# Attention with chunk selection and a gated MLP block: weight loads tied to pairs 2 and 3, six weight and four activation transposes moved from DMA to TensorE, evacuations on either engine, a new order table

## The chip, the cores and the metric

One NeuronCore of a Trainium2 chip runs the whole program. The metric is device time in microseconds (us) from the first to the last instruction and what the launch adds. The kernel before took 241.61 us as the median of 3 runs (240.44 to 242.94).

## The reference

```python
# attention: B=4, H=8, S=768, D=64, chunk=32 (24 chunks), top_k=6
k_min, k_max = per-chunk minimum and maximum of k over its 32 rows
ub = np.sum(np.maximum(q * k_min, q * k_max), axis=-1)          # a bound for each query and chunk
ub = np.where(causal, ub, -1e9)
top_chunks = np.argsort(ub, axis=-1)[..., -top_k:]
scores = np.where(sel & causal_by_position, (q @ k.T) / sqrt(D), -1e9)
attn_out = softmax(scores) @ v
# gated MLP on x = attn_out as (B, S, 512)
h = gelu_tanh(x @ w_in)                                        # w_in 512 x 1024
u, v = h[..., :512], h[..., 512:]
v_n = (v - mean) / sqrt(var + 1e-6) * g_ln                     # over the 512 features
v_s = einsum('ts,bsd->btd', w_sg, v_n) + b_sg[None, :, None]   # w_sg 768 x 768, over positions
out = x + (u * v_s) @ w_out                                    # w_out 512 x 512
```

Inputs and output are float32; the kernel multiplies in bf16 behind the selection.

## The kernel before, in words

**Units of work.** The 32 heads (4 batches of 8) go in 16 pairs, p0 to p15; four pairs are a batch, and each batch ends in the MLP. A function makes named operations, and each is a few instructions on one engine. For a pair: `lk`, `lq`, `lv` load k, q, v of one head each by DMA from SyncE (192 KB, in pieces of 256 bytes, at most four of them in flight). `kt` and `qt` are TensorE transposes into PSUM. `kn` and `kx` (VectorE) take the chunk minima and maxima, `ke`, `ka`, `kb` and `qe` (ScalarE) copy the transposed k and q out of PSUM, `qr` is the positive part of q, and `qa`, `qb`, `qc` (GpSimd) are bf16 casts of q. `ub` multiplies for the bounds of one selection group: pair 0, pair 1, then pairs two at a time. `ut`, `uc`, `um`, `ud`, `uq` (all VectorE) transpose, cut off what is not causal, find the sixth largest, compare, and transpose back: they make the mask. `s` multiplies scores into one of two PSUM tiles PSC, `e` (ScalarE) takes the exponential out of it, `af` (GpSimd) cuts the diagonal, `pv` and `pd` multiply by v, and `xr`, `xs` (VectorE) normalise into XS. Pairs 0 to 3 (batch 0) use tiles of both heads (`s0.3`, `e0.3`); later heads have three tiles each (`s8h.0`). There the mask rows reach QA and QB by small DMAs `d`.

**The MLP of a batch.** `xt` makes x^T of 128 features from XS: a DMA transpose on SyncE (line 824), except for the last of batch 3, which TensorE makes (line 833). Then come `hv` and `gv` (v half and gelu), `bs`, `ba`, `re`, `rp`, `vh` (the norm), `hu` and `gu` (u half and gelu), `pt` (the product with w_sg), `vs`, `gm` (scaling and gating; `gm` on GpSimd or VectorE), `ou`, `oa`, `os` (out product, residual, store).

**Weights.** `win` (w_in, 4 DMAs, line 489), `wsg` (w_sg, 6, line 493) and `wo` (w_out, 4, line 500) are loads with a cast that GpSimd issues. `wsgT` (line 496) are six DMA transposes on SyncE that make w_sg^T. The w_sg staging tile lies in the buffer that the first gelu writes.

**Order.** `ORDER` is a table written out by hand: one list of all operations, from which each engine takes its own in turn. `kt0.0:0` names a PSUM buffer, `qr0@act` an engine other than the default. An engine runs its list strictly in order, and waits on semaphores for what an operation reads, for the users of the PSUM buffer that it takes over, and for tiles to come free. The instructions that follow in its list wait with it, on SyncE's and GpSimd's DMA queues too. Operations that share a PSUM tile run in the order in which the program made them. `FILL` puts a number of multiplications of a zero tile `warm` (line 984) before a TensorE operation that waits; they need only the PSUM buffer, and keep TensorE at work.

The plan has one stretch that repeats: attention for the next pairs runs between the products of the MLP of the batch before. Batch 0 has no such partner: until the first `hv0`, TensorE has only batch 0's attention and the first operations of pairs 4 to 8.

## Time and profile before

| | |
|---|---|
| runs, median (lowest to highest) | 241.61 us (240.44 to 242.94) |
| the profiled execution, its own time | 239.15 us |
| its span, first to last instruction | 237.4 us |
| busy: TensorE, VectorE, ScalarE, GpSimd | 211.3, 175.1, 167.3, 107.1 us |
| granted TensorE clock, mean | 0.995 |

Busy time is the time in which at least one instruction of the engine ran; matmuls are pipelined, so TensorE's includes their tails, and it includes the `warm` multiplications. PEld is TensorE's weight load. In the views, a line number is that of the printed kernel; tiles are named by the program, and as `KP` lies in the buffer of `uT`, and the w_sg staging in that of `vgb`, their rows carry those names.

### The profile page before, as it was taken

The numbers are of one execution on the slowest core, as the hardware profiler recorded it, in microseconds if no ns is written. First come the engines' busy times: TensorE is split into PE (matmuls) and PEld (weight loads), VectorE is DVE, ScalarE is ACT, GpSimd is POOL, SyncE is SP. The second block draws the span as 40 slices with busy tenths as digits, with TensorE's granted clock in tenths as the row PEclk, the third lists the DMA queues.
The fourth block names the chain that finished last, engine by engine and source line by source line (L and its number), as shares of the span: only waits on it lengthen the run. The fifth ranks groups of instructions, "written<-read, shape, count | busy, mean of one in ns | idle before, by whom it ended". The sixth has DMA issues, their size and how long they took to land.

```text
span 237.4 us, 6067 instructions
## 1 busy us (share of the span) xinstructions
PE 211.3 (89%) x2329; PEld 133.2 (56%) x2351; DVE 175.1 (74%) x543; ACT 167.3 (70%) x264; POOL 107.1 (45%) x147
## 2 busy tenths in 40 slices
...
GB/s 160 207 219 192 204 207 209 200 195 171 123 209 177 182 199 147 81 95 216 195 227 177 186 26 82 134 166 69 4 94 30 92 123 79 196 140 0 0 90 176
DMA packets 100541, 33.72 MB, mean 142 GB/s; under 512 B 93985, under 2 KB 96801, under 8 KB 100513
## 3 DMA queue, kind: packets, MB, share of 16 engines
...
q8 instruction: 18, 0.29, 0.5%
...
## 4 chain that ended last, share of the span: by engine, by line
PE 65%; DVE 14%; ACT 12%; DMA 4%; issue 2%; POOL 0%; POOLq 0%; SPq 0%; DVEq 0%; ACTq 0%
PE PSG L909 11%; PE PSC L775 9%; PE PSG L889 9%; PE PSG L854 8%; PE PSG L932 5%; PE PSG L796 5%; DVE W L535 4%; PE PSG L528 3%; ACT E L745 3%; PE PSG L623 3%; PE PSG L984 3%; PE PSG L561 3%; ACT E L779 2%; DMA xT<-XS 2%; ACT qT L567 2%
## 5 line engine op out<-in xcount | busy, mean ns | idle before, releaser
L779 ACT ACTIVATE E<-PSC 128x1024 bf16<-128x1024 f32 (+1 forms) x72 | 62.8, 916 | 11.3 <-PE PSC L775 10.9
L681 POOL TENSOR_SCALAR_AFFINE_SELECT E<-E 128x768 bf16<-128x768 bf16 (+3 forms) x40 | 29.3, 745 | 27.1 <-ACT E L779 19.3
L535 DVE TENSOR_REDUCE W<-PSG 128x12 f32<-128x384 f32 x64 | 34.4, 547 | 9.2 <-PE PSG L528 8.6
L909 PE MATMUL PSG<-wsgT,vhat 128*128 128x384 bf16 x192 | 35.2, 326 | 1.5 <-DVE XS L815 1.4
L745 ACT ACTIVATE E<-PSC 128x1024 bf16<-128x1024 f32 (+3 forms) x26 | 21.7, 858 | 7.5 <-PE PSC L735 7.2
L916 DVE SCALAR_TENSOR_TENSOR vsT<-PSG,glnT,bsgbc 128x384 f32<-128x384 f32 x32 | 18.9, 604 | 9.1 <-PE PSG L909 7.4
L909 PEld LDWEIGHTS PSG<-wsgT,vhat 128*128 128x128 bf16 x192 | 17.9, 98 | 12.7 <-DVE XS L815 1.6
L586 POOL CAST vx<-vn 128x768 bf16<-128x768 f32 x16 | 13.4, 843 | 22.2 <-DMA vn<-in_v_dram 21.9
L854 PE MATMUL PSG<-winb,xT 128*128 128x512 bf16 x93 | 21.9, 379 | 1.4 <-ACT qT L567 0.9
L922 POOL TENSOR_TENSOR uT<-vsT,uT 128x384 bf16<-128x384 f32 x17 | 16.0, 947 | 14.9 <-DVE vsT L916 14.8
L889 PE MATMUL PSG<-xT,winb 128*128 128x384 bf16 x128 | 22.3, 326 | 0.4 <-DMA xT<-XS 0.3
L932 PE MATMUL PSG<-woutb,uT 128*128 128x512 bf16 x86 | 21.7, 379 | 0.9 <-POOL uT L922 0.3
L874 POOL TENSOR_TENSOR rstd<-rstd,neghalf 128x3 f32<-128x3 f32 x8 | 7.6, 948 | 32.9 <-DVE rstd L870 32.9
L796 PE MATMUL PSG<-vx,E 128*128 128x65 bf16 x480 | 19.7, 194 | 1.5 <-DVE osb L939 1.4
L567 ACT ACTIVATE qT<-PSG 128x384 f32<-128x384 f32 x32 | 15.3, 496 | 8.2 <-PE PSG L561 7.8
L775 PE MATMUL PSC<-QA,KA 96*128 96x128 bf16 (+2 forms) x168 | 19.3, 246 | 1.7 <-ACT qT L567 0.9
L939 DVE TENSOR_TENSOR osb<-PSG,XS 128x512 f32<-128x512 f32 x24 | 16.2, 686 | 5.7 <-DMA out_dram<-osb 4.4
L796 PEld LDWEIGHTS PSG<-vx,E 128*128 128x128 bf16 x480 | 17.7, 98 | 4.0 <-DVE osb L939 1.8
L813 DVE RECIPROCAL rden<-PSG 128x6 f32<-128x6 f32 x32 | 6.0, 189 | 18.3 <-PE PSG L804 18.2
L775 PE MATMUL PSC<-QB,KB 128*128 128x128 bf16 (+2 forms) x168 | 19.3, 246 | 0.1
L864 DVE BATCH_NORM_STATS2 stats<-vgb 128x6 f32<-128x512 f32 x24 | 15.9, 682 | 4.0 <-ACT vgb L859 3.9
L984 PE MATMUL PSG<-warm 128*128 128x512 bf16 x45 | 14.0, 430 | 5.3 <-ACT qT L567 1.6
...
## 6 DMA issues: line engine op xcount, KB each, us to landing
...
```

The lines of the kernel that those rows point to most:

```text
L535: P.op(f"k{'nx'[m]}{p}.{hf}", "dve", lambda d, t=t, m=m, op=op, hf=hf: d.tensor_reduce(W[w][:, m, 12 * hf:12 * hf + 12], t.ap()[:, 0:TG].r ...
L567: P.op(f"qe{p}.{hf}", "act", lambda e, t=t, cs=cs: e.activation(qT[w][:, cs], t.ap()[:, 0:TG], ACTF.Copy), writes=[("qT", w, hf)], ps=[t], ...
L681: P.op(f"af{h}.{r}", "pool", lambda g, ev=ev, cnt=cnt: g.affine_select(ev, ev, pattern=[[0, cnt], [1, 128]], compare_op=ALU.is_ge, fill=0. ...
L745: P.op(f"e{p}.{c}", "act", lambda e, t=t, o0=o0, nn=nn: e.activation(E[:, slot:slot + 2, o0:o0 + nn], t.ap().rearrange("p (i x) -> p i x", ...
L775: r = e.matmul(t.ap()[:, o:o + n], kt_[rows, 128 * kb:128 * kb + 128], qt_[rows, q0:q0 + n], start=True, stop=True, skip_group_check=True)
L779: P.op(f"e{h}h.{c}", "act", lambda e, t=t, c0=c0, c1=c1: e.activation(E[:, es, c0:c1], t.ap()[:, 0:c1 - c0], ACTF.Exp, scale=SCALE), write ...
L796: r = e.matmul(t.ap()[:, 65 * qb:65 * qb + 65], E[:, es, a:a + 128], vx[w][:, kb, i, :], start=first, stop=False, skip_group_check=True)
L854: r = e.matmul(t.ap()[:, 0:F], xT[s][:, dk, 128 * qt:128 * qt + 128], winb[:, dk, F:DFF], start=(dk == 0), stop=(dk == NDK - 1))
L889: r = e.matmul(t.ap()[:, 0:TG], winb[:, dk, 128 * fb:128 * fb + 128], xT[s][:, dk, TG * tg:TG * tg + TG], start=(dk == 0), stop=(dk == NDK ...
L909: r = e.matmul(t.ap()[:, 0:TG], vhat[s][:, sb, 128 * fb:128 * fb + 128], wsgT[:, sb, TG * tg:TG * tg + TG], start=(sb == 0), stop=(sb == N ...
L932: r = e.matmul(t.ap()[:, 0:DM], gT[s][:, fb, 128 * qt:128 * qt + 128], woutb[:, fb, :], start=(fb == 0), stop=(fb == NF - 1))
L984: return e.matmul(o.ps[0].ap()[:, 0:512], warm[:, 0:128], warm[:], start=True, stop=True, skip_group_check=True)
```

## The change

What it does:

- **Weight loads.** `win`, `wsg`, `wo`, `bsg`, `gln` are now made after pair 3's operations and each waits for one: `win0` and `win1` for `qc2`, `win2` and `win3` for `qc3`, `wsg0` to `wsg5` for the exponentials `e2.0` to `e2.5`, `wo`, `bsg`, `gln` for those of pair 3.
- **w_sg^T by TensorE.** Each of six staged blocks of w_sg goes through six transposes into a PSUM tile (`wt`), and a VectorE copy of 128x768 bf16 (`we`). The six DMA transposes on SyncE are gone. The staging lies in `vhat[1]` and `xT[1]`, buffers of batch 1.
- **x^T of batch 0 by TensorE.** `XPE` now lists the four `xt0`, so four more DMA transposes are gone. The copy out of PSUM is one operation of 768 columns (`xe`), on VectorE or ScalarE, where batch 3's last had been one of 384 on each.
- **Evacuations.** `ke`, `ka`, `kb`, `qe`, `xe` may run on either engine. In the new table 15 of them that ScalarE had run stand on VectorE (`ka6.1`, `kb5.1` and `ka6.0` ahead of the first MLP), and `xe0.1` on ScalarE. Of the 16 `qr`, 9 are ScalarE's, where there were 13. The `gm` on VectorE fall from 15 to 10, those on GpSimd rise from 17 to 22.
- **Fillers.** `FILL` has 26 multiplications at 7 places, where there were 65 at 22.
- **Order.** `ORDER` is new throughout. The costs of operations that the diff also changes are used by nothing that runs here, and `NWIDE` is 0, so `halves` gives the blocks of before.

```diff
-FILL = {"kt0.0": 8, "qt0.0": 3, "ub0": 5, "qt1.0": 1, "kt2.0": 3, "ub1": 6, "s0.3": 2, "qt2.1": 3, "s1.0": 1, 
-    "s1.2": 2, "s2.5": 4, "s2.2": 1, "s3.0": 2, "qt7.1": 2, "pv6": 8, "ub4": 3, "qt8.1": 2, "qt8.0": 1, "qt6.0": 1, 
-    "hu0.00": 2, "s8h.0": 4, "hu3.11": 1, }
+FILL = {"kt1.1": 11, "kt0.0": 3, "qt0.1": 3, "ub0": 4, "ub1": 1, "pv2": 2, "ub8": 2, }
...
-    XPE = ((B - 1, NDK - 1),)
+    XPE = [(0, dk) for dk in range(NDK)] + [(B - 1, NDK - 1)]
...
-        wsgf = vgb[:].rearrange("p a b -> p (a b)").bitcast(BF16)[:, 0:NT * S].rearrange("p (a b) -> p a b", b=S)
+        wsgf = [vhat[1][:].rearrange("p a b -> p (a b)")[:, S * j:S * j + S] for j in range(3)] + \
+               [xT[1][:, dk, :] for dk in range(1, 4)]
...
-            P.op(f"wsgT{j}", "sp", lambda e, j=j: e.dma_start_transpose(
-                out=wsgT[:, :, 128 * j:128 * j + 128], in_=wsgf[:, j, :]),
...
+            P.op(f"xe{b}.{dk}", "dve", lambda d: d.tensor_copy(xT[s][:, dk, :], t.ap(BF16)[:, 0:S]), writes=wr, ps=[t],
+                 cost=(480, 560), prio=prio, alt={"act": dict(fn=lambda e: e.activation(
+                     xT[s][:, dk, :], t.ap(BF16)[:, 0:S], ACTF.Copy), cost=c_act(S))})
...
+        def weights():
+            for j in range(NDK):
+                P.op(f"win{j}", "pool", lambda g, j=j: g.dma_start(
+                    winb[:, j, :], bass.AP(w_in.tensor, 128 * DFF * j, [[DFF, 128], [1, DFF]])),
+                    writes=[("winb", j)], dma=f"winb{j}", cost=(600, 1750), prio=80.0 + 10 * j,
+                     after=[f"qc{2 + j // 2}"])
+            for j in range(NT):
+                P.op(f"wsg{j}", "pool", lambda g, j=j: g.dma_start(
+                    wsgf[j], bass.AP(w_sg.tensor, 128 * S * j, [[S, 128], [1, S]])),
+                    writes=[("wsgf", j)], dma=f"wsgf{j}", cost=(600, 1300), prio=120.0 + 5 * j,
+                     after=[f"e2.{j}"])
+                t = ps_g.tile()
+
+                def tr(e, t=t, j=j):
+                    for sb in range(NT):
+                        r = e.matmul(t.ap(BF16)[:, 128 * sb:128 * sb + 128], wsgf[j][:, 128 * sb:128 * sb + 128],
+                                     identB[:], is_transpose=True)
+                    return r
+                P.op(f"wt{j}", "pe", tr, reads=[("wsgf", j), "identB"], alloc=[t], cost=(335, 499),
+                     prio=150.0 + 5 * j)
+                P.op(f"we{j}", "dve", lambda d, t=t, j=j: d.tensor_copy(
+                    wsgT[:, :, 128 * j:128 * j + 128],
+                    t.ap(BF16)[:, 0:S].rearrange("p (a b) -> p a b", b=128)), writes=[("wsgT", j)], ps=[t],
+                    cost=(480, 560), prio=150.0 + 5 * j)
```

**The start, on VectorE.** In the table of before the tile `warm`, for which the first fillers wait, is VectorE's second row:

```order
L468 MEMSET W 128x2x8 x2
L452 MEMSET warm 128x256
L535 TENSOR_REDUCE W<-PSG 128x12 x2
L468 MEMSET W 128x2x8
L535 TENSOR_REDUCE W<-PSG 128x12
```

In the table of the change the same engine begins so (`J` sums the identity, which GpSimd makes):

```order
L470 MEMSET W 128x2x8
L473 MEMSET vx 128x12
L460 TENSOR_REDUCE J<-identF 128x32
L470 MEMSET W 128x2x8
L473 MEMSET vx 128x12
L470 MEMSET W 128x2x8
L473 MEMSET vx 128x12
L454 MEMSET warm 128x256
L538 TENSOR_REDUCE W<-PSG 128x12 x8
```

`warm` moved from behind two zeroings to behind seven instructions, and all eight reductions of pairs 1 and 0 now stand ahead of anything of pair 0's selection.

**The start of batch 0's MLP, on TensorE.** Before, from the last transposes ahead of it (`kn`, `qn` transposes, fillers from `warm`, the bounds `qT,W`) to `hu0.00` and the `hv0` (lines 889 and 854):

```order
L984 MATMUL PSG<-warm 128x512 x3
L623 MATMUL PSG<-qT,W 32x288 x8
L623 MATMUL PSG<-rT,W 32x288 x8
L984 MATMUL PSG<-warm 128x512 x2
L561 MATMUL PSG<-identF,qn 128x128 x3
L984 MATMUL PSG<-warm 128x512
L561 MATMUL PSG<-identF,qn 128x128 x3
L984 MATMUL PSG<-warm 128x512
L561 MATMUL PSG<-identF,qn 128x128 x3
L984 MATMUL PSG<-warm 128x512 x2
L889 MATMUL PSG<-xT,winb 128x384 x4
L854 MATMUL PSG<-winb,xT 128x512 x16
```

The same engine in the table of the change, from the last diagonal product `pd7` on (line 840 is `xt0.3`, line 970 a `wt`, line 781 scores of heads 8 and 10):

```order
L810 MATMUL PSG<-vx,E 128x65 x6
L629 MATMUL PSG<-qT,W 32x288 x8
L629 MATMUL PSG<-rT,W 32x288 x8
L840 MATMUL PSG<-identB,XS 128x128 x6
L781 MATMUL PSC<-QA,KA 128x128 x6
L781 MATMUL PSC<-QA,KA 128x256
L970 MATMUL PSG<-identB,vhat 128x128 x6
L781 MATMUL PSC<-QA,KA 128x256 x2
L781 MATMUL PSC<-QA,KA 128x128
L860 MATMUL PSG<-winb,xT 128x512 x4
L895 MATMUL PSG<-xT,winb 128x384 x4
```

The fillers between are gone. In front of the first `hv0` now stand the third selection group's bounds, the last x^T transposes, one of the six `wt`, and score tiles of heads 8 and 10; the transposes of q of pair 8, one `hu` and two `hv` moved behind it.

**The weight loads, on GpSimd.** Before, the first of them stand right after pair 0's diagonal cuts (`vgb` is w_sg's staging, `winb` w_in):

```order
L493 DMA vgb<-in_moe_w_sg_dram 128x768
L489 DMA winb<-in_moe_w_in_dram 128x1024
L493 DMA vgb<-in_moe_w_sg_dram 128x768
L681 AFFINE_SELECT E<-E 128x384
L681 AFFINE_SELECT E<-E 128x256
L493 DMA vgb<-in_moe_w_sg_dram 128x768
```

In the change nine of the ten loads of w_in and w_sg stand close together, from behind `vc3`, the third cast of v (staging now in `vhat` and `xT`):

```order
L962 DMA vhat<-in_moe_w_sg_dram 128x768
L585 CAST QA<-qT 64x768
L962 DMA vhat<-in_moe_w_sg_dram 128x768
L587 CAST QB<-qT 64x768
L957 DMA winb<-in_moe_w_in_dram 128x1024
L962 DMA xT<-in_moe_w_sg_dram 128x768 x2
L687 AFFINE_SELECT E<-E 128x768
L592 CAST vx<-vn 128x12x64
L585 CAST QA<-qT 64x768
L962 DMA vhat<-in_moe_w_sg_dram 128x768
L957 DMA winb<-in_moe_w_in_dram 128x1024
L687 AFFINE_SELECT E<-E 128x768
L957 DMA winb<-in_moe_w_in_dram 128x1024 x2
```

Five blocks of w_sg and all of w_in are asked for in one row of nine issues, after the first exponential of pair 2 at the earliest.

## Rows read from the trace of the kernel before

**Rows 1.** The page: the span, first to last instruction.

```profile
span 237.4 us, 6067 instructions
```

**Rows 2.** Busy us by stretch: length, PE, PEld, DVE, ACT, POOL, granted clock, DMA.

```profile
0.00:17.70 17.70, 14.80 (x140) 8.50 (x144) 10.22 (x47) 6.13 (x11) 2.18 (x8) 1.00 1.19 195
17.70:40.10 22.40, 18.45 (x314) 11.88 (x317) 15.53 (x69) 17.46 (x31) 17.47 (x31) 1.00 1.03 202
40.10:68.20 28.10, 22.79 (x291) 13.41 (x296) 15.82 (x56) 21.90 (x37) 13.25 (x21) 1.00 1.18 177
68.20:120.20 52.00, 46.29 (x510) 30.31 (x514) 43.82 (x119) 40.38 (x64) 30.80 (x39) 1.00 0.83 167
120.20:167.50 47.30, 45.94 (x516) 31.10 (x518) 40.63 (x113) 42.34 (x68) 17.41 (x20) 1.00 0.57 126
167.50:207.10 39.60, 38.65 (x440) 25.70 (x442) 29.83 (x103) 30.47 (x43) 20.21 (x24) 1.00 0.34 87
```

**Rows 3.** The same view of the fillers (line 984) alone: PE, PEld, clock, DMA.

```profile
0.00:68.20 68.20, 15.98 (x52) 5.53 (x60) 1.00 1.13 190
```

**Rows 4.** Instructions in order of time, the start: start, length, engine, line, xcount.

```profile
1.31 3.59 PE L984 MATMUL PSG<-warm 128*128 128x512 bf16 x8 [1.31 <-DVE warm L452]
1.75 0.29 POOL L454 TENSOR_SCALAR_AFFINE_SELECT identF<-identF 128x128 f32<-128x128 f32 x1
4.70 1.49 PE L528 MATMUL PSG<-identF,kn 128*128 128x128 f32 x6
6.84 0.82 PE L561 MATMUL PSG<-identF,qn 128*128 128x128 f32 x6
7.13 0.36 DVE L458 TENSOR_REDUCE J<-identF 128x32 f32<-128x128 f32 x1
```

**Rows 5.** The same view: the first exponentials of pair 0 and of pair 2.

```profile
17.73 1.02 ACT L745 ACTIVATE E<-PSC 128x1024 bf16<-128x1024 f32 x1 [2.70 <-PE PSC L735]
40.06 1.73 ACT L745 ACTIVATE E<-PSC 128x1024 bf16<-128x1024 f32 x2 [2.97 <-PE PSC L735]
```

**Rows 6.** Busy us by stretch, columns as in rows 2: ScalarE's attention of batch 0.

```profile
17.70:57.00 39.30, 32.09 (x494) 19.79 (x500) 23.57 (x87) 33.48 (x56) 26.43 (x45) 1.00 1.13 194
```

**Rows 7.** The chain that ended last: start, us, what; its longest piece.

```profile
60.58 5.39 DMA xT<-XS
```

**Rows 8.** Groups of instructions: busy us, mean ns, idle time before them.

```profile
L779 ACT ACTIVATE E<-PSC 128x1024 bf16<-128x1024 f32 (+1 forms) x72 | 62.8, 916 | 11.3 <-PE PSC L775 10.9
L535 DVE TENSOR_REDUCE W<-PSG 128x12 f32<-128x384 f32 x64 | 34.4, 547 | 9.2 <-PE PSG L528 8.6
L745 ACT ACTIVATE E<-PSC 128x1024 bf16<-128x1024 f32 (+3 forms) x26 | 21.7, 858 | 7.5 <-PE PSC L735 7.2
L567 ACT ACTIVATE qT<-PSG 128x384 f32<-128x384 f32 x32 | 15.3, 496 | 8.2 <-PE PSG L561 7.8
L545 ACT ACTIVATE KA<-PSG 64x384 bf16<-64x384 f32 x24 | 11.4, 481 | 5.5 <-DVE W L535 5.4
L573 ACT ACTIVATE rT<-qT 128x576 f32<-128x576 f32 x13 | 8.9, 687 | 0.1
```

**Rows 9.** Groups: x^T of batch 3 by TensorE, its copy on VectorE.

```profile
L833 PE MATMUL PSG<-identB,XS 128*128 128x128 bf16 x6 | 0.5, 221 | 0.0
L838 DVE COPY xT<-PSG 128x384 bf16<-128x384 bf16 x1 | 0.4, 358 | 0.6 <-PE PSG L833 0.6
```

**Rows 10.** One line's instructions: w_sg loads (first), w_in loads (second).

```profile
DMA to landing us min/median/max: 4.6/6.1/8.7
DMA to landing us min/median/max: 4.3/7.3/8.6
```

**Rows 11.** In order of time: VectorE operations with two SBUF inputs.

```profile
86.77 3.52 DVE L922 TENSOR_TENSOR uT<-vsT,uT 128x384 bf16<-128x384 f32 x1
97.42 2.86 DVE L652 TENSOR_TENSOR Dn<-U,m 128x288 bf16<-128x288 f32 x1
221.97 0.56 DVE L922 TENSOR_TENSOR uT<-vsT,uT 128x384 bf16<-128x384 f32 x1
```

352 lines of the change are left out of this document (186 added, 166 removed).

## The prediction

> **What bounds the kernel now.** I read the busy time by stretch first, with borders at operations whose start I looked up: the first exponential (17.7 us), pair 2's first exponential (40.1), and the first `hv` of each batch (68.2, 120.2, 167.5, 207.1). From 68.2 to 207.1 TensorE is the bound: it is busy 46.3 of 52.0, 45.9 of 47.3 and 38.7 of 39.6 us, and all but 5 of the 65 fillers stand ahead of it [rows 2]. Ahead of 68.2 it isn't. There TensorE is busy 56.0 us, but 16.0 of these are fillers, so real work fills 40 of 68 us [rows 2, 3]. No other engine is full there either: VectorE is busy 41.6 us, ScalarE 45.5, GpSimd 32.9 [rows 2]. This start is a chain that passes from engine to engine, and it is where the change can give something.
>
> The reader is to see three things in it. First, ScalarE is the engine nearest to its limit while it has batch 0's exponentials: 33.5 of the 39.3 us from 17.7 to 57.0, 85% [rows 6]. Second, of the 5.8 us that it idles, 2.97 are one wait, for pair 2's first scores, which wait for that group's mask from VectorE [rows 5]. Third, from 57.0 on the attention of batch 0 is over, and the chain goes through the DMA transpose of the last x^T for 5.39 us, its longest piece [rows 7].
>
> **The change part by part.**
>
> *The lead-in: 0.4 us later.* The first fillers now wait for a `warm` that stands behind `J`, which needs GpSimd's identity. The identity was there at 2.04 us behind a large zeroing; behind a small one I take 1.7. `J` takes 0.36, and the memsets and `warm` some 0.5 (an estimate: two memsets and `warm` were done by 1.31). The fillers then start at about 2.6 where they did at 1.31 [rows 4]. There are 11 where there were 8. The next transposes began 3.39 us after the first of eight, so 0.43 apiece; 512 columns in 0.43 us is the lower level, 1.2 GHz. The six transposes of q at 6.84 take 0.82 us where k's six took 1.49, so the clock had risen by then [rows 4]. Eleven at 0.43 end at 7.3, and the first transposes come 2.6 us later than at 4.70. Against that, four reductions of pair 1 no longer stand inside pair 0's selection: 4 x 0.547 = 2.2 us [rows 8]. Net +0.4; bounds -0.4 (the clock rises during the fillers) and +2.6 (nothing is won back). The first exponential comes at 18.1.
>
> *From the first exponential to the first `hv`: 4.3 us shorter.* It takes 50.5 us now. In the new order the score tile `s10h.2` stands just before `hv0.0` on TensorE and needs the buffer that `e10h.1` frees, so ScalarE's list up to there is on the path whatever the rest does. Counted in the table: 26 exponentials of pairs 0 to 3, 21.7 us; 4 of heads 8 and 10 at 62.8/72 = 0.87, 3.5; 14 copies of 384 (`ke`, `qe`) at 15.3/32 = 0.48, 6.7; 12 half copies (`ka`, `kb`) at 11.4/24 = 0.475, 5.7; 4 `qr` at 8.9/13 = 0.68, 2.7 [rows 8]; `xe0.1` some 0.8, near an exponential. Sum 41.1. The idle time: 2.9 us of small waits as now, and half of the 2.97 [rows 5, 6], since ScalarE has pair 4's and 5's copies to do meanwhile: 4.4. Then `s10h.2` and the start of `hv`, 0.7. Together 46.2 instead of 50.5. Bounds: no idle time at all, -8.7; the share of 85% [rows 6], 41.1/0.85 = 48.4 + 0.7, -1.4.
>
> The 5.39 us of the DMA transpose [rows 7] aren't subtracted as such. What replaces them is six transposes, 0.5 us [rows 9], and one copy of 768 columns, all under ScalarE's list. The copy isn't in the trace. For 384 it took 0.358 [rows 9]; 768 take between that and 0.72, and I take 0.55. Nine such copies on VectorE and ten groups of transposes on TensorE are new: up to 6.5 us and 5 us, seven and nine of them ahead of `hv0.0`. TensorE has 24 fillers there instead of 60, so they fit. VectorE's load ahead of `hv0.0` becomes 41.6 + 7 x 0.55 + three moved copies (0.36 to 0.55 each) + two `qr` (about 0.5 each), near 48 of the 56 us from its first reduction: high, and under ScalarE's.
>
> *The DMA side: nothing.* Ten DMA transposes leave SyncE's queue, ahead of loads of pairs 7 to 9 that they had held. The loads of weights move later: `wsg0` can't issue before `e2.0`, about 42 us. Nine issues with two cuts and four casts between them are 15 operations; GpSimd took 17.47 us for 31 in the stretch to 40.1 [rows 2], 0.56 each, so 8.4 us. One cut waits for pair 2's last exponential, so I put the last issue at 52. A w_in load lands 4.3 to 8.6 us after its issue [rows 10], so the last by 61, and that is ahead of `hv0.0` at 64. `wt0` on TensorE, at about 49.5, waits for `wsg0`, which lands at 47 to 51 [rows 10]; behind it stands the score tile `s3.3`, for which ScalarE waits. That is worth 0 to 1.5 us and is inside the idle time taken.
>
> *Behind the first `hv`: 0.5 us shorter.* Heads 8's and 10's scores and the bounds of group 6 have moved ahead; two `qt`, one `hu`, two `hv` and one `wt` behind. By length these cancel within a microsecond, so the work left for the bounding engine is the same. Five fillers become two: three by 0.21 (half of 0.43, at the upper level, 2.4 GHz), 0.6, of which I take 0.5. VectorE gets the moved copies in batches 1 and 2 and loses five `gm`; it is busy 40.6 of 47.3 us there now [rows 2], which leaves room. I take the 169.2 us as they are.
>
> **Sum.** +0.4 - 4.3 - 0.5 = -4.4 us. The span goes from 237.4 [rows 1] to 233.0, and the profiled execution's own 239.15 to 234.75. The median of the runs shown, 241.61, lies 2.46 above that execution; against it the sum gives 237.2, which I predict: 1.8% faster.
>
> **The rivals.**
>
> *The start gains nothing.* VectorE at 48 of 56 us could make ScalarE wait as often as now. With the idle share at 15% and the lead-in's whole 2.6 us: +2.6 - 1.4 - 0.5 = +0.7, 242.3. For it speaks that this plan asks both engines to be nearly full at once; against it, that the 85% had a single wait of 2.97 in it [rows 5].
>
> *The weights land late.* If the casts and cuts between the issues wait for pair 2's last exponential, the last w_in load issues some 3 us later and lands at 64 in the worst case; with `wt0` and `wt2` holding the scores, 2 to 4 us go back: 239 to 241. Against it: 8.6 is the longest landing of a w_in load, the median is 7.3 [rows 10].
>
> *GpSimd and VectorE in each other's way: slower.* At 86.77 a `gm` on VectorE took 3.52 us where 0.56 is usual, and at 97.42 a compare of 288 columns took 2.86 [rows 11]; both have two SBUF inputs, and GpSimd ran without a pause beside them. The table gives GpSimd five more `gm`, and VectorE more work in the same stretches. One such collision costs 2.3 to 3.0 us on a path that VectorE holds. Two more of them cancel the gain; four give 237.2 + 4 x 2.7 = 248. It decides where GpSimd reads SBUF back to back while VectorE starts such an operation. Against it: five `gm` fewer on VectorE are five fewer that can be caught, and the new copies read PSUM.
> The Trainium skill ("SBUF — State Buffer", Who interferes with whom) says that a VectorE instruction with two SBUF inputs and a GpSimd instruction that reads SBUF exclude each other, and that the second to come waits out the first. The two long rows agree with it. By that rule alone the new copies out of PSUM with one input cost GpSimd nothing, and the sum would be the one above.
>
> *The clock falls.* With 24 fillers ahead of `hv0.0` instead of 60, TensorE may idle more in the start. At the lower level six transposes took 1.49 instead of 0.82 us; 20 us of TensorE's work at that price would add up to 16 us, 253. Against it: the granted clock was 1.00 in every stretch up to 207 us [rows 2], and the new plan packs TensorE's 40 us of work into a shorter start.
>
> **How the numbers follow.** Forecast 0.60, no gain 0.20, weights 0.06, collisions 0.10, clock 0.04. Faster by over 1% is below 239.2: most of the forecast (0.57) and part of two rivals (0.07), 0.64. Within 1%, 239.2 to 244.0, about what a measurement of this kernel can tell from no change: 0.03 + 0.15 + 0.02 + 0.03 = 0.23. Slower: 0.13. The range: downwards the bound of no idle time with the clock's early rise, -0.4 - 8.7 - 0.5 = -9.6, gives 232, and 230 if one of the two collisions of rows 11 goes as well; upwards the first rival's 242.3 and a little of the others, 243.5. The forecast's own range is 232 to 240.5.
>
> **What would show it right or wrong.** In the profile after: the first `warm` filler near 2.6 us and the first exponential near 18; ScalarE busy over 88% from there to `hv0.0`; `hv0.0` near 64; no DMA transpose in the chain before 70; about 169 us behind `hv0.0`. It is wrong if `hv0.0` comes at 67 or later, if TensorE waits for w_in or w_sg, if VectorE shows more operations with two SBUF inputs of over 2 us, or if the granted clock falls below 1.00 before the end.

## The result

| | before | after |
|---|---|---|
| runs, median (lowest to highest) | 241.03 us (238.84 to 242.94) | 227.81 us (226.17 to 229.75) |
| ratio after / before, 95% interval | | 0.946 (0.930 to 0.961) |
| the profiled execution: span | 237.4 us | 224.5 us |
| first exponential, `hv0.0`, `hv1.0`, `hv2.0`, `hv3.0` start at | 17.7, 68.2, 120.2, 167.5, 207.1 | 17.8, 59.0, 104.6, 154.2, 194.6 |

The change makes the kernel 5.4% faster. The forecast was 1.8%, 237.2 us with a range from 230: the direction was right, and the time lies below the range. The forecast span was 233.0 against 224.5 measured, so 8.5 us were missed. Some executions of a kernel take over 1.5% more than its fastest one: medians have them in, ratios, here and below, leave them out, and there is no ratio where one execution was left.

The page of the kernel after, and its busy time by stretch (length, PE, PEld, DVE, ACT, POOL with instructions, granted clock, DMA share and GB/s). The borders are again the first exponential, pair 2's first exponential, and `hv0.0` to `hv3.0`:

```profile
span 224.5 us, 6115 instructions
```

```profile
0.00:17.76 17.76, 11.93 (x123) 6.94 (x126) 11.41 (x48) 6.88 (x14) 8.40 (x19) 1.00 1.19 198
17.76:38.50 20.74, 19.59 (x329) 13.68 (x328) 18.13 (x78) 18.40 (x32) 8.79 (x18) 0.92 0.96 195
38.50:59.03 20.53, 20.42 (x362) 14.14 (x361) 18.62 (x60) 19.86 (x30) 16.73 (x24) 1.00 0.93 163
59.03:104.60 45.57, 43.55 (x467) 29.66 (x470) 39.11 (x100) 37.76 (x62) 25.41 (x31) 1.00 0.91 172
104.60:154.20 49.60, 46.55 (x525) 31.84 (x524) 46.18 (x142) 36.68 (x55) 26.98 (x31) 1.00 0.67 151
154.20:194.60 40.40, 38.58 (x438) 25.33 (x438) 29.75 (x104) 31.96 (x42) 20.25 (x23) 1.00 0.29 77
```

Beside [rows 2] the reader sees where the time went. From the first exponential to `hv0.0` there are 41.3 us where there were 50.5, and TensorE, ScalarE and VectorE are busy 40.0, 38.3 and 36.8 of them. Before, TensorE was idle or on fillers for 16.7 of the 50.5 us (41.2 busy, 7.5 of them on the 32 fillers behind 17.7), and now for 1.6. The stretch from `hv0.0` to `hv1.0` takes 45.6 instead of 52.0 us, with TensorE idle 2.0 instead of 5.7. The next one is 2.3 us longer, the one after it 0.7. The fillers ahead of `hv0.0` take 6.92 us, where they took 15.98 [rows 3]. There are 24 now and there were 60: the trace lacks records of some products (22 and 52 are in it), and the second count of a row, of weight loads, has them all:

```profile
0.00:59.03 59.03, 6.92 (x22) 2.36 (x24) 0.97 1.02 185
```

One correction to the borders themselves. In the order of before `hv0.0` is the third `hv` of its batch; `hu0.00` starts at 66.02 and `hv0.3` at 66.52, and batch 1 starts with `hv1.2` at 119.07. By the first `hv` of any number the start gained 7.5 us, the next stretch 7.0, and the one behind it lost 1.2. The findings below hold by either border; the numbers go by `hv0.0` to `hv3.0`, as the prediction's did.

### The profile page after: what moved, and what is told of

Its sections match the earlier page's. It is cut to its first block, busy times and chain, and to the rows that moved or that the text cites. A ratio compares the mean times of both kernels' runs of the same rounds, so it can differ in the third digit from the quotient of the medians.

```text
span 224.5 us, 6115 instructions
## 1 busy us (share of the span) xinstructions
PE 205.1 (91%) x2357; PEld 134.4 (60%) x2372; DVE 182.3 (81%) x566; ACT 158.7 (71%) x245; POOL 113.2 (50%) x152
## 3 DMA queue, kind: packets, MB, share of 16 engines
q1 hardware_dynamic: 90496, 28.62, 59.4%
q0 software_dynamic: 2016, 2.75, 8.2%
## 4 chain that ended last, share of the span: by engine, by line
PE 63%; DVE 20%; DMA 5%; ACT 4%; issue 3%; POOL 2%; SPq 1%; POOLq 0%
PE PSC L781 11%; PE PSG L915 11%; PE PSG L938 8%; PE PSG L860 7%; PE PSG L523 7%; PE PSG L802 5%; PE PSG L895 4%; DMA QB<-Dt 3%; DVE m L653 3%; DVE stats L870 2%; PE PSG L629 2%; DVE Dn L658 2%; DVE W L538 2%; PE PSG L1032 2%; DVE vhat L885 2%
## 5 line engine op out<-in xcount | busy, mean ns | idle before, releaser
L687 POOL TENSOR_SCALAR_AFFINE_SELECT E<-E 128x768 bf16<-128x768 bf16 (+3 forms) x40 | 28.8, 726 | 24.1 <-ACT E L785 13.2
L928 POOL TENSOR_TENSOR uT<-vsT,uT 128x384 bf16<-128x384 f32 x22 | 20.9, 956 | 18.4 <-DVE vsT L922 18.2
L915 PEld LDWEIGHTS PSG<-wsgT,vhat 128*128 128x128 bf16 x192 | 18.1, 98 | 10.4 <-DVE vhat L885 0.5
L895 PE MATMUL PSG<-xT,winb 128*128 128x384 bf16 x128 | 23.1, 326 | 0.0
L592 POOL CAST vx<-vn 128x768 bf16<-128x768 f32 x16 | 13.9, 875 | 13.5 <-DMA vn<-in_v_dram 13.4
L865 ACT ACTIVATE vgb<-PSG 128x512 f32<-128x512 f32 x24 | 13.7, 598 | 8.2 <-PE PSG L860 8.1
L571 ACT ACTIVATE qT<-PSG 128x384 f32<-128x384 f32 x30 | 13.8, 490 | 7.9 <-PE PSG L523 7.9
L821 DVE TENSOR_TENSOR XS<-PSG,rden 128x384 bf16<-128x384 f32 x32 | 17.4, 550 | 0.7
L895 PEld LDWEIGHTS PSG<-xT,winb 128*128 128x128 bf16 x128 | 12.4, 98 | 8.7 <-ACT vgb L865 0.3
```

Source lines behind the costliest of these rows:

```text
L687: P.op(f"af{h}.{r}", "pool", lambda g, ev=ev, cnt=cnt: g.affine_select(ev, ev, pattern=[[0, cnt], [1, 128]], compare_op=ALU.is_ge, fill=0. ...
L895: r = e.matmul(t.ap()[:, 0:TG], winb[:, dk, 128 * fb:128 * fb + 128], xT[s][:, dk, TG * tg:TG * tg + TG], start=(dk == 0), stop=(dk == NDK ...
L915: r = e.matmul(t.ap()[:, 0:TG], vhat[s][:, sb, 128 * fb:128 * fb + 128], wsgT[:, sb, TG * tg:TG * tg + TG], start=(sb == 0), stop=(sb == N ...
L928: return d.tensor_tensor(gT[s][:, fb, TG * tg:TG * tg + TG], vsT[vs][:], uT[s][:, fb, TG * tg:TG * tg + TG], op=ALU.mult)
```

## The experiments

Names that begin with a are the kernel after with an edit, names that begin with b the kernel before with one. Ratios are to the kernel before on the same chip.

| | median us (lowest to highest) | ratio (95%) | span | clock |
|---|---|---|---|---|
| after, again | 228.12 (227.10 to 229.51) | 0.947 (0.936 to 0.959) | 225.6 | 0.994 |
| a_xtdma | 235.19 (233.83 to 236.01) | 0.974 (0.969 to 0.979) | 233.8 | 0.967 |
| a_wsgdma | 234.06 (228.96 to 237.48) | - | 233.0 | 0.978 |
| a_bothdma | 238.62 (235.43 to 240.69) | 0.981 (0.961 to 1.001) | 235.6 | 0.964 |
| b_xtpe | 247.69 (244.34 to 252.07) | 1.017 (1.009 to 1.025) | 242.6 | 0.987 |
| b_wsgpe | 244.68 (242.35 to 248.41) | 1.013 (1.008 to 1.018) | 240.8 | 1.000 |
| b_gm | 238.62 (237.45 to 238.77) | 0.987 (0.983 to 0.991) | 237.0 | 0.996 |
| b_lead | 243.49 (241.43 to 249.27) | 1.006 (1.001 to 1.011) | 239.7 | 0.961 |
| b_lv3 | 245.41 (240.17 to 246.90) | - | 243.9 | 0.968 |
| a_s8late | 234.03 (233.42 to 235.56) | 0.970 (0.962 to 0.978) | 231.9 | 0.978 |
| a_actevac | 230.85 (229.73 to 232.07) | 0.954 (0.946 to 0.963) | 230.3 | 0.979 |
| a_fill | 225.83 (224.48 to 227.07) | 0.935 (0.927 to 0.944) | 225.4 | 0.989 |
| a_vh | 225.94 (225.26 to 226.76) | 0.939 (0.934 to 0.944) | 224.2 | 0.996 |
| a_lead | 226.60 (226.48 to 226.93, one execution of 410.76 left out) | 0.942 (0.936 to 0.948) | 224.7 | 0.984 |
| a_vhwsg4 | 225.96 (225.05 to 228.76) | 0.937 (0.925 to 0.949) | 227.0 | 0.974 |
| a_best | 221.22 (220.66 to 221.73) | 0.918 (0.909 to 0.927) | 219.3 | 0.998 |

### The order and the two sets of transposes

**a_xtdma**: x^T of batch 0 by DMA again, in the new order.

```diff
-    XPE = [(0, dk) for dk in range(NDK)] + [(B - 1, NDK - 1)]
+    XPE = [(B - 1, NDK - 1)]
-... xt0.0:1 ... xe0.0 ... xt0.3:3 ... xe0.3
+... xt0.0 ... xt0.3
```

> The changed kernel with one part undone: the four x^T of batch 0 are DMA transposes on SyncE again, at the places in the order where TensorE had them; the four copies are gone. Theory A (the start's gain comes from the packed order, in which TensorE is busy 40.0 of the 41.3 us from the first exponential to the first hv; the x^T transposes on TensorE only keep the last link short): the last DMA transpose can start at 57.4 us and takes 5.4 us as in the kernel before, so the first hv comes near 63 instead of 59.0, and the whole is 3 to 4 us slower than the change, near 231. Theory B (taking the DMA transposes out of the path gives most of the start's gain): the first hv goes back to 66 to 68, 7 to 9 us slower, near 236. Theory C (a DMA transpose is hidden anyway): within 1 us of the change, 227 to 229.

`hv0.0` came at 66.3, and the whole is 7 us slower than the change: B's number, but made of more than the transpose. One piece of the chain of waits, then busy time by stretch:

```profile
61.77 4.52 DMA xT<-XS
```

```profile
60.00:66.40 6.40, 1.59 (x26) 1.01 (x18) 4.23 (x26) 3.63 (x5) 3.57 (x5) 0.88 1.26 174
66.40:72.00 5.60, 5.26 (x15) 2.17 (x17) 0.88 (x2) 0.60 (x1) 0.00 (x0) 0.53 1.06 166
```

The transpose itself takes 4.5 us, near the 5.4 that A priced, but it starts at 61.8 and not at 57.4. Batch 0's last `xs` ends at 59.95, where it ended at 57.36 in the change (the first exponential came 0.75 us later in this execution, and TensorE had waited 1.4 us for a load of q), and from there the transpose stood 1.8 us in SyncE's queue, behind a load of v (2.76 us of that queue) and the transpose ahead of it (1.95). Then TensorE, which has no fillers at this place in the new order, is busy only 1.59 of 6.40 us while it waits, and in the next 5.6 us its granted clock is 0.53, mostly the lower level: the `hv` that waited for x^T then run at about half speed. `hv0.0` to `hu0.11` takes 12.6 us instead of 10.2.

**a_wsgdma**: w_sg^T by DMA again, in the new order.

```diff
-                P.op(f"wt{j}", "pe", tr, ...)
-                P.op(f"we{j}", "dve", ...)
+                P.op(f"wsgT{j}", "sp", lambda e, j=j: e.dma_start_transpose(
+                    out=wsgT[:, :, 128 * j:128 * j + 128], in_=wsgf[j]), ...)
```

> The changed kernel with one part undone: w_sg^T is made by six DMA transposes on SyncE again, where TensorE had its six groups; their copies on VectorE (six of 0.54 us) and the groups on TensorE (six of about 0.5 us) are gone. Theory A (TensorE and VectorE are the bound ahead of the first hv, SyncE's queue isn't): 0 to 2 us faster than the change ahead of the first hv, since five groups and five copies fall away there, unless the loads of pairs 7 to 9 come late behind the transposes; 226 to 229. Theory B (six DMA transposes in the queue and on the transfer engines delay the loads of k, q and v): the chain goes through DMA or SyncE ahead of 75 us, and the whole is 2 to 5 us slower, 230 to 233.

In the execution shown, B's mechanism at more than B's price: `hv0.0` at 69.7. In the chain the longest piece is a mask row's transfer for head 8, and TensorE's longest wait is for it (waits: for whom, in all, times, longest):

```profile
48.15 13.75 DMA QA<-Dt
```

```profile
PE PSC L781 <- DMA QA<-Dt: 10.5, 1, 10.5
```

It was issued right behind the first of the DMA transposes (1.31 us of SyncE's queue, just ahead of it in the chain); that transpose landed at 60.8, 14.0 us after its issue, and the row at 61.9. The score tile `s8h.1`, which the new order puts ahead of batch 0's last products, waited for it until 61.97, and those products stand behind it on TensorE. In the change the same row, issued at 46.85, landed after 4.4 us. But of this kernel's four executions one took 228.96, as long as the change takes, and three 233.4 to 237.5; the one shown is of these. So what this set costs by DMA is anything from nothing to some 9 us, and its price isn't settled.

**b_xtpe** and **b_wsgpe**: each set on TensorE, in the order of before.

```diff
+    XPE = tuple((0, dk) for dk in range(NDK)) + ((B - 1, NDK - 1),)
-... xt0.0 ... xt0.1 ... xt0.2 ... xs7 ka7.0 kn7.1 ub4:30 xt0.3
+... xt0.0:2 xe0.0 ... xt0.1:2 xe0.1 ... xt0.2:0 xe0.2 ... xs7 xt0.3:0 xe0.3 ka7.0 kn7.1 ub4:30
```

> The kernel before with one part of the change: the four x^T of batch 0 by TensorE, in the order of before, each copied by VectorE in one piece; the bf16 identity is made earlier. Theory A (the order is what gains; in the order of before other things end almost as late as the last DMA transpose: the PSUM buffer of the first hu comes free at 65.03, where the transpose ended at 65.97): 0 to 1.5 us faster than before, 239.5 to 241. Theory B (the DMA transpose's 5.39 us at the end of the chain are the loss): 4 to 6 us faster, 235 to 237.

```diff
-            P.op(f"wsgT{j}", "sp", lambda e, j=j: e.dma_start_transpose(...))
+            P.op(f"wt{j}", "pe", tr, reads=[("wsgf", j), "identB"], alloc=[t])
+            P.op(f"we{j}", "dve", ...)
-... wsgT1 ... wsgT5
+... wt1:2 we1 ... wt4:2 we4 ... wt3:0 we3 ... wt0:1 ... wt2:2 ... wt5:1 ... we0 ... vh0.5 we2 we5
```

> The kernel before with one part of the change: w_sg^T by TensorE (six groups of six transposes, six copies of 128x768 on VectorE, staging in buffers of batch 1), in the order of before; the six DMA transposes leave SyncE's queue. Theory Q (the DMA transposes in SyncE's queue, each held until its block of w_sg has landed, hold the loads and mask rows behind them, and this alone costs the start): the loads of pairs 5 to 9 go out earlier, the first hv comes 2 to 4 us earlier, the whole is 2 to 4 us faster, 237.5 to 239.5. Theory K (only the order that uses the free queue gains from it): between 1 us faster and 2 us slower than before.

Both alone are slower than before, by 1.7% and 1.3%: nearest to theories A and K, with a loss that A didn't have. (Each set was tried at one place in the old order; what it would cost at a better one isn't shown.) In b_xtpe the last x^T is there within 1.2 us of XS instead of 5.4, and nothing comes of it, since `hu0.00` needs a PSUM buffer that the copies of pair 7's keys free, and these stand behind the group's bounds. Two pieces of its chain, the last x^T transposes and those bounds:

```profile
62.39 0.51 PE PSG L833 x6
63.55 1.28 PE PSG L623 x32
```

From the start of `xs7` to the first `hv` it takes 7.2 us, 6.5 before: the bounds now wait until x^T has left their PSUM buffer. That is 0.7 of the 5.2 us by which this execution's span is longer; 1.8 are lost ahead of `xs7` already, in part where TensorE waits 0.7 us for the copy of an earlier x^T, and the rest behind the first `hv`, for reasons that no run shows. In b_wsgpe the first of the last three copies stands 0.56 us ahead of the last four `vhat`, and these then meet GpSimd's casts (VectorE in order of time; the same four took 2.50 us in the kernel before):

```profile
78.18 0.56 DVE L506 COPY wsgT<-PSG 128x768 bf16<-128x768 bf16 x1 [1.03 <-PE PSG L502]
78.65 3.76 DVE L890 TENSOR_SCALAR vhat<-vgb,mv,rstd 128x512 bf16<-128x512 f32 x4
```

The last two copies stand behind them, and TensorE waits 1.8 us for the last.

**a_bothdma**: both sets by DMA, in the new order (the two edits above together).

> The changed kernel with both sets of transposes back on the DMA engines: x^T of batch 0 and w_sg^T, in the places of the new order. With x^T alone put back the first hv came at 66.3, with w_sg^T alone at 69.7 in the profile, against 59.0. Theory N (the new order is worth nothing without the free queue): the first hv at 68 to 76, the whole 234 to 241. Theory O (the order carries the gain, and each part only its own few us): first hv at 66 to 68, the whole 229 to 233.

238.6 us: N's time. The mask row that took 13.75 us in a_wsgdma is late here too (from the chain, then TensorE's longest wait):

```profile
51.22 8.31 DMA QA<-Dt
```

```profile
PE PSC L781 <- DMA QA<-Dt: 5.5, 1, 5.5
```

In a_xtdma, with x^T alone by DMA, the same row took 4.2 us, about as in the change: of the two sets it is that of w_sg^T that makes it late.

With an interval from 0.961 to 1.001 the new order alone (with its fillers, weight loads and moved copies) is worth some 2%, and it may be nothing or 4%. So the square reads: transposes alone, at the places tried, +1.7% and +1.3%, order alone -1.9%, all together -5.3%. None of the three makes the gain by itself. As the traces show it, the order uses what the transposes free (a queue with nothing slow ahead of the mask rows, and a short last link), and only then does it pay.

### Behind the first hv

**b_gm**: the gating product that collided at 86.77 [rows 11] goes to GpSimd, in the kernel before.

```diff
-... kb8.0 xr9 gm0.02@dve
+... kb8.0 xr9 gm0.02
```

> The kernel before with one word of the table changed: the gating gm0.02, which took 3.52 us on VectorE at 86.8 us, stands on GpSimd. Theory C (the stretch from the first hv of batch 0 to that of batch 1 gained its 6.5 us because two VectorE operations with two SBUF inputs no longer waited for GpSimd): 2 to 3 us faster than before, 238 to 239, and TensorE's wait of 1.40 us at 91 us is gone. Theory D (that stretch gained because the scores of heads 8 and 10 and a selection group had moved ahead of it, and the collision is hidden): within 0.7 us of before.

C: 3.1 us faster by the runs (interval 2.2 to 4.1 us of 241.65). The stretch from `hv0.0` to `hv1.0`, and the other collision of [rows 11], which stays:

```profile
70.15:119.78 49.63, 45.61 (x509) 30.36 (x513) 39.94 (x118) 40.62 (x65) 31.67 (x40) 1.00 0.87 174
```

```profile
96.86 2.86 DVE L652 TENSOR_TENSOR Dn<-U,m 128x288 bf16<-128x288 f32 x1
```

The stretch is 2.4 us shorter than in [rows 2], and the list of TensorE's waits has the one for XS no longer. A single instruction on the wrong engine cost over 1% of the kernel. (The start of that execution is 2 us longer than in the one shown of before; it isn't touched by the edit.)

**a_s8late**: the scores of heads 8 and 10 behind the first MLP products again.

```diff
-... s8h.1:0 ... e8h.1 ... s10h.2:1 hv0.0:3 ... pv8:3 gu0.01
+... hv0.0:3 ... gu0.01 s8h.1:0 s8h.2:1 e8h.1 s10h.0:0 ... s10h.2:1 e8h.0 af8.0 e10h.2 pv8:3
```

> The changed kernel with the scores, exponentials and diagonal cuts of heads 8 and 10 (six score tiles, about 3 us of TensorE; six exponentials, 5.7 us of ScalarE) and the product pv8 moved from before the first hv to behind the last gu of batch 0. Theory A (TensorE's work is what counts from the first exponential on; moved work only shifts the borders): the first hv comes 2 to 4 us earlier, near 56, that of batch 1 within 1.5 us of 104.6, the whole within 1.5 us of the change. Theory E (that the scores can run ahead of the first hv, into what TensorE and ScalarE have free there, is where the stretch behind the first hv gained): the first hv a little earlier, but that of batch 1 later by 2 to 5 us, and the whole 2 to 5 us slower, 230 to 233.

E, and clearly: 6 us slower. `hv0.0` comes at 59.4, not at 56, although four exponentials and six score tiles have left ScalarE's and TensorE's lists ahead of it. Stretches of this kernel (to `hv0.0`, and where the moved block now stands):

```profile
17.76:59.40 41.64, 39.07 (x666) 26.07 (x667) 37.09 (x139) 36.37 (x59) 25.44 (x42) 0.96 0.92 175
76.00:90.00 14.00, 13.21 (x123) 9.28 (x122) 7.78 (x15) 9.52 (x13) 9.36 (x12) 0.80 0.21 39
```

So ScalarE's list up to `e10h.1` doesn't set `hv0.0` alone: the chain through the third selection group's bounds and the copy of the last x^T ends at the same time without it, and the early scores fill room that is free beside that chain. Two pieces of the chain, and a wait of TensorE behind `hv0.0`:

```profile
57.10 1.28 PE PSG L629 x32
58.89 0.45 DVE xT L845
```

```profile
PE PSC L781 <- ACT E L785: 2.5, 2, 2.2
```

Behind `hv0.0` the moved scores cost their full length and more, since TensorE waits 2.5 us for exponentials there and its clock falls to 0.80 over 14 us. In the kernel before the same scores could not run early: the mask rows of pair 4 were issued at 69.6 us there (`d4.00`), and at 45.6 after the change.

**a_actevac**: the 15 copies on VectorE back on ScalarE.

```diff
-... ka6.1@dve ... kb5.1@dve ... ka12.1@dve ...
+... ka6.1 ... kb5.1 ... ka12.1 ...
```

> The changed kernel with the 15 PSUM copies (ka, kb, qe) that the table gives to VectorE back on ScalarE, in the same places of the order; three of them stand ahead of the first hv. Theory A (both engines have room for these copies, 0.48 us each on ScalarE and 0.55 on VectorE): the start 0 to 1.5 us longer, the rest within 1 us; 227 to 230. Theory G (the choice of engine carries a good part of the gain): 3 us or more slower, above 231.

Between A and G: some 2 to 3 us slower by the runs. The three copies in the start cost about 0.8 us. The stretch from `hv1.0` to `hv2.0` takes 52.9 instead of 49.6 us, and TensorE's waits there have ScalarE's key copies among them (stretch, then waits: for whom, in all, times, longest):

```profile
105.62:158.55 52.93, 49.27 (x532) 32.70 (x524) 41.12 (x130) 41.64 (x67) 27.06 (x31) 0.97 0.62 142
```

```profile
PE PSG L523 <- ACT KB L551: 0.9, 2, 0.7
PE PSG L802 <- ACT KB L551: 0.7, 1, 0.7
```

Not all of the 3.3 us is the copies' own: behind a wait for a mask row, which the change has as well, the clock is 0.67 from 120 to 125 us here and 1.00 in the change. a_fill below, with the copies on VectorE, has such a fall at the same place and loses 2.4 us by it and by waits.

### Fillers and the clock

**b_lead**: only the 8 fillers of the first transposes are left in the kernel before.

```diff
-FILL = {"kt0.0": 8, "qt0.0": 3, ... "hu3.11": 1, }
+FILL = {"kt0.0": 8}
```

> The kernel before with the 8 fillers of its first transposes alone; the other 57 are taken out. Theory F (fillers stood in the way: the start of the change gained because 36 of them are gone): 1 to 4 us faster than before, 237 to 240. Theory H (they filled waits and kept the clock): without them TensorE idles some 16 us more in the start, the granted clock falls below 1.00 there, and the whole is 2 to 8 us slower, 243 to 249.

H, but smaller than its price: 0.6% slower.

```profile
17.70:40.10 22.40, 18.79 (x332) 12.35 (x326) 15.03 (x72) 17.17 (x30) 15.67 (x29) 0.96 1.02 195
40.10:68.20 28.10, 20.00 (x270) 12.67 (x267) 14.73 (x52) 19.07 (x32) 14.95 (x23) 0.87 1.21 170
```

The clock falls to 0.96 and 0.87, where TensorE has little to do anyway. The 57 fillers did not stand in the way, and their going is not where the change gained.

**a_fill**: six fillers ahead of `s0.4` in the change.

```diff
-FILL = {..., "ub1": 1, "pv2": 2, "ub8": 2, }
+FILL = {..., "ub1": 1, "s0.4": 6, "pv2": 2, "ub8": 2}
```

> The changed kernel with six more fillers, ahead of the first score tile s0.4, where TensorE idles 1.86 us before the clock falls to 0.50 from 19 to 22.5 us. Theory H (the idle stretch makes the clock fall): the clock stays at 1.00 from 17 to 26 us, the scores of pair 0 and the transposes of pair 2 take half as long there, and the whole is 1 to 2 us faster, 225.5 to 227, with less spread. Theory I (the fall there costs nothing since ScalarE is the bound): within 0.5 us.

The change has a fall of the clock of its own. TensorE waits 1.9 us for pair 0's mask (first row), and at 20 us the clock is at the lower level (stretches of the kernel after):

```profile
PE PSC L734 <- DVE Dt L663: 2.7, 2, 1.9
```

```profile
17.76:22.00 4.24, 4.24 (x57) 3.10 (x54) 3.59 (x25) 3.34 (x5) 0.00 (x0) 0.64 0.97 186
20.00:22.00 2.00, 2.00 (x22) 1.61 (x19) 1.83 (x5) 1.37 (x3) 0.00 (x0) 0.50 0.84 188
```

With the fillers it is 1.00 there, and TensorE starts 76 instead of 57 matmuls in the same 4.24 us:

```profile
17.76:22.00 4.24, 4.24 (x76) 2.99 (x74) 3.72 (x26) 3.82 (x6) 0.50 (x2) 1.00 0.85 167
```

`hv0.0` comes 1.25 us earlier, at 57.8, and the runs are some 2 us faster, though the intervals overlap: H. In the execution shown the gain is lost again: the clock falls at another wait, for a mask row behind `hv1.0`, and the stretch to `hv2.0` takes 52.1 instead of 49.6 us:

```profile
103.33:155.43 52.10, 48.78 (x531) 33.13 (x524) 46.85 (x143) 37.51 (x56) 26.89 (x31) 0.97 0.64 143
```

Neither fall comes in every execution: the one shown of "after, again" kept 1.00 from 17 to 25 us behind the same wait of 1.9 us, and the change kept it behind `hv1.0`.

### Waits that the change left, and a faster kernel

**b_lv3**: a miss. Pair 3's second v load earlier in the kernel before.

```diff
-... lv3.0 xs0 ... kb6.0 lv3.1 ka5.1 ...
+... lv3.0 lv3.1 xs0 ... kb6.0 ka5.1 ...
```

> The kernel before with one load moved: lv3.1, the second half of pair 3's v, stands on SyncE's queue right behind lv3.0 (30.8 us) and not at 50 us. Before, pv6 started at 56.88, just after the cast of that v on GpSimd ended at 56.72, and in another run of the same start at 59.24 after 59.12. Theory V (the late v of pair 3 holds the last products of batch 0's attention): the cast ends by 52, pv6 starts when the exponentials allow, near 56.6, xs7 ends by 60.5 in every run, and the whole is 0.5 to 2.5 us faster than before. Rival: another load moves behind it and is late in its place; within 0.7 us of before.

The cast of that v didn't come earlier but at 60.96, since it stands behind a diagonal cut on GpSimd. Instead a load that had to go behind it was late: TensorE waited 3.4 us for pair 6's k, and its clock fell to 0.50 for 6 us.

```profile
PE PSG L528 <- DMA kn<-in_k_dram: 3.4, 1, 3.4
```

```profile
50.00:56.00 6.00, 6.00 (x51) 2.53 (x52) 1.09 (x2) 3.79 (x8) 2.97 (x5) 0.50 1.08 173
```

In this execution theory V falls and the rival holds. That k was asked for only 1 us later than before, so why it landed so late isn't settled, nor what of this kernel's time is that wait and what the clock. Three of the four executions took 245.1 us or more, this one among them; the fourth took 240.17, a microsecond under the kernel before, and what V is worth where no load is late isn't shown.

**a_vh**: GpSimd does nothing while VectorE makes the last four `vhat` of batch 0.

```diff
+        P.by_name["iB0"].deps[P.by_name["vh0.4"].idx] = 1
         P.arrange(ORDER)
```

> The changed kernel with one wait added: GpSimd's copy for pair 4's key rows and its two casts of pair 6's q, which ran from 70.57 to 73.35 us, wait for vh0.4, so that GpSimd does nothing while VectorE makes batch 0's last four vhat. Theory J (VectorE's normalisation waits for GpSimd's casts: the four took 4.04 us here and 1.92 in batch 2): the four take 1.9 to 2.4 us, the first pt comes 1.5 to 2 us earlier, and the whole is 1 to 2 us faster, 225.5 to 227. Rival (the long four are VectorE's own, or another wait of 2 us stands behind): within 0.5 us.

J's mechanism, and by the runs a time in J's range (225.94), but the trace doesn't show J's gain. VectorE in order of time in the kernel after, and in a_vh:

```profile
70.04 4.04 DVE L885 TENSOR_SCALAR vhat<-vgb,mv,rstd 128x512 bf16<-128x512 f32 x4 [1.01 <-POOL rstd L880]
```

```profile
69.77 1.92 DVE L885 TENSOR_SCALAR vhat<-vgb,mv,rstd 128x512 bf16<-128x512 f32 x4 [1.01 <-POOL rstd L880]
```

The span is 224.2 against 224.5, and the first `pt` comes 0.55 us earlier, not 2: now TensorE waits 1.4 us for the last block of w_sg, as it had waited 1.2 before the edit (a_vh's chain):

```profile
66.80 5.75 DMA xT<-in_moe_w_sg_dram
```

The Trainium skill ("SBUF — State Buffer", Who interferes with whom) names tensor_scalar among the VectorE operations that can hold the port pair shared with GpSimd, by its mode and not by a second SBUF input. The trace agrees that one large input is enough: these four have no other, and lose 2.1 us to GpSimd's copy and two casts. In which mode they ran it doesn't show.

**a_vhwsg4**: and that block asked for earlier.

```diff
-... gu0.21 wsg4 vh0.1 ...
+... win3 wsg4 uq4.1 ...
```

> The changed kernel with GpSimd's copy and two casts waiting for vh0.4, as in a_vh, and the last block of w_sg, wsg4, asked for right behind win3 (about 50 us) instead of at 67. In a_vh the four vhat took 1.91 us instead of 4.04, but the first pt came only 0.55 us earlier, since wt4 then waited 1.4 us for that block, which landed at 72.7. Theory J (the collision cost 2 us, hidden by the load behind it): the first pt comes 1.0 to 1.8 us earlier than in a_vh, near 72, and the whole is 1 to 2 us faster than the change. Rival (a third wait of the same length stands behind): within 0.5 us of a_vh.

From `vh0.5`, the first of the four, to the first `pt` it takes 2.3 us now, where it took 4.1 after the change and 3.8 in a_vh: J. The profiled execution has `hv0.0` at 62.8, 4 us later than a_vh: its clock falls to 0.50 at 22 to 24 us and is 0.66 in the mean from 40 to 50, ahead of what the edit touches, so "near 72" can't be read off; by the runs it is 225.96, no faster than a_vh within their spread.

**a_lead**: fillers earlier and fewer.

```diff
-zA3 lk1.0 W00 vx13 J0 ... vx10 warm0 lk0.0 ...
+zA3 lk1.0 warm0 W00 vx13 J0 ... vx10 lk0.0 ...
-FILL = {"kt1.1": 11, ...
+FILL = {"kt1.1": 8, ...
```

> The changed kernel with warm zeroed first on VectorE and 8 fillers ahead of the first transposes instead of 11. The fillers then run from 1.3 to 4.8 us, as in the kernel before, and the first transposes come near 4.8 instead of 6.25. Theory L (the 11 late fillers hold the first transposes, whose k has landed by about 4.4 us): the first exponential comes 0.8 to 1.5 us earlier, the whole 0.5 to 1.5 us faster, unless the clock has not risen by then. Rival (the later k and q loads set the lead-in): the first exponential within 0.4 us, the whole within 0.5 us.

Theory L in the lead-in: the first transposes at 4.64 instead of 6.25, the first exponential 1.0 us earlier. But behind the same wait for the mask, 1.9 us, the clock falls again and stays down longer, and `ub2` comes at 31.28, as in the change (31.12):

```profile
16.75:22.75 6.00, 6.00 (x60) 4.24 (x58) 4.09 (x25) 4.22 (x6) 0.83 (x3) 0.50 0.90 190
```

**a_best**: a_fill, a_lead and a_vhwsg4 together, and one mask row earlier.

```diff
-... d9.01 hu1.30:0 vh1.0 d8.11 ... d8.01 ... re1.1 d9.00 ...
+... d9.01 hu1.30:0 vh1.0 d9.00 d8.11 ... d8.01 ... re1.1 ...
```

> The changed kernel with the edits of a_fill, a_lead and a_vhwsg4 together, and the mask row d9.00, for which the score tile s18h.0 waits at 115 to 119 us, asked for two places earlier on SyncE's queue. If each does what it did alone: the first exponential at 16.8 with the clock at 1.00 (1.0 us and 1.2 us), the first pt 1.5 us earlier, the score tile 1.2 us earlier: 3 to 5 us faster than the change, 222 to 224.5. Rival (gains ahead of 105 us are lost again in the wait for mask rows at 115 and 128 us): 1 to 2 us faster.

221.22 us, 0.918 of before: faster than both kernels, and 6.9 us less than the 228.12 of "after, again" (6 less than its two faster executions). The sum of the parts was 3 to 5. Its four executions lie within 1.1 us of each other, with a clock of 0.998 or 0.999. From the first exponential to `hv0.0`, and on to 102 us:

```profile
16.76:56.17 39.41, 38.94 (x690) 26.70 (x687) 36.28 (x137) 37.97 (x62) 26.17 (x43) 1.00 1.00 193
```

```profile
56.00:102.00 46.00, 45.68 (x483) 30.66 (x481) 39.33 (x106) 39.67 (x64) 24.68 (x30) 1.00 0.93 184
```

TensorE is busy 99% of both.

## Why the prediction was right or wrong

**What failed.** Two terms of the sum make up nearly all of the 8.5 us: the start, 46.2 us where 41.3 were measured (4.9), and what lies behind `hv0.0`, 0.5 us to gain where 3.7 were gained (3.2). In the first, ScalarE's list was put at 41.1 us and took 37.9, its idle time at 4.4 and was 2.75. In the second, the moves of work across `hv0.0` were taken to cancel, and no collision was taken to go; the first stretch behind `hv0.0` lost 6.5 us. The last 0.3 are the lead-in.

**What bounds the kernel.** Right in the place (the start, and a chain from engine to engine). Behind `hv0.0` the forecast called TensorE the bound and took the 169.2 us "as they are"; but TensorE idled 5.7 of the first 52.0 us there by [rows 2], and that could be won.

**The lead-in, +0.4.** Near enough, by luck: the first exponential is at 17.76, +0.03. The fillers start at 2.54 as said, but the 11 take 3.87 us instead of 4.7, since the clock rises while they run (the bound of -0.4 named it). Against that, less was won back than the 2.2 us of four reductions: the first transposes came 1.55 us later than before, so 1.5 were. In the execution shown of "after, again" the fillers take 4.88 us, the first transposes come at 7.21 as forecast, 1.3 us are won back, and the first exponential is at 18.95, +1.2. TensorE in order of time in the kernel after [rows 4], and the fillers in the other:

```profile
2.54 3.87 PE L1032 MATMUL PSG<-warm 128*128 128x512 bf16 x11 [2.54 <-DVE warm L454]
6.25 0.82 PE L523 MATMUL PSG<-identF,kn 128*128 128x128 f32 x6
```

```profile
2.54 4.88 PE L1032 MATMUL PSG<-warm 128*128 128x512 bf16 x11 [2.54 <-DVE warm L454]
```

**From the first exponential to `hv0.0`, -4.3.** It was -9.2. The forecast end was 18.1 + 46.2 = 64.3, the measured one 59.03. The 5.3 us between are 0.3 of the lead-in, 3.2 of ScalarE's list (41.1 forecast, 37.9 busy), 1.6 of its idle time (4.4 forecast, 2.75), and 0.1 of the last step. ScalarE up to `e10h.1`'s end, by stretch and by group:

```profile
17.76:58.40 40.64, 39.38 (x680) 27.22 (x678) 36.12 (x136) 37.89 (x61) 24.89 (x41) 0.96 0.95 178
```

```profile
L751 ACT ACTIVATE E<-PSC 128x1024 bf16<-128x1024 f32 (+3 forms) x26 | 21.6, 862 | 4.1 <-PE PSC L741 4.0
L571 ACT ACTIVATE qT<-PSG 128x384 f32<-128x384 f32 x10 | 4.7, 492 | 0.0
L785 ACT ACTIVATE E<-PSC 128x1024 bf16<-128x1024 f32 (+1 forms) x4 | 3.8, 938 | 0.2 <-PE PSC L781 0.2
L551 ACT ACTIVATE KB<-PSG 64x384 bf16<-64x384 f32 x6 | 2.9, 485 | 0.2
L551 ACT ACTIVATE KA<-PSG 64x384 bf16<-64x384 f32 x6 | 2.9, 477 | 0.0
L579 ACT ACTIVATE rT<-qT 128x576 f32<-128x576 f32 x4 | 2.7, 682 | 0.0
L543 ACT ACTIVATE uT<-PSG 128x384 bf16<-128x384 f32 x4 | 1.9, 494 | 0.0
L846 ACT ACTIVATE xT<-PSG 128x768 bf16<-128x768 bf16 x1 | 0.8, 818 | 0.0
```

The groups add up to 41.3, the forecast's 41.1 (by lengths, count times mean, it is 42.4, as a group's busy time leaves out the overlap inside it), and the engine is busy 37.9: neighbours overlap, by 4.5 us over 61 instructions. Adding up single instructions or groups overstates a full engine; the busy time of a stretch is the right term, and the forecast had it at hand ([rows 6] gives 33.5 for 56). The Trainium skill ("ScalarE: Activation LUTs", What ACT_TABLE_LOAD costs) has back-to-back activations overlap by about 0.093 us. The trace agrees: 43 of the 61 start before the one ahead of them has ended, by 0.10 us in the mean.

The deeper fault is the claim that this list is on the path "whatever the rest does". a_s8late takes four exponentials off it, and `hv0.0` stays at 59.4. Several chains end together there, and 93% busy ScalarE is one of them. The forecast's idle share was also read from an order in which TensorE and ScalarE waited for each other; the new one leaves 7%.

That the 5.39 us of the DMA transpose "aren't subtracted as such" was right for the order of before, where b_xtpe finds them worth less than nothing. In the new order a_xtdma has `hv0.0` 7.3 us later with DMA transposes: there the short last link is a condition of the gain.

**The DMA side, nothing.** Its own sum held: the nine loads were issued by 50.4 (52 forecast) and `wt0` ran at 45.9. What it lacked is what stands on SyncE's queue behind the DMA transposes: the mask rows of heads 8 to 11. With w_sg^T by DMA one of them takes 13.75 us (a_wsgdma) and 8.31 (a_bothdma) where the change has 4.4, and TensorE waits 10.5 and 5.5 us for it. Without those transposes the scores of heads 8 and 10 run 22 to 34 us earlier than before, and a_s8late shows that having them ahead of `hv0.0` is worth 6 us. The forecast saw both moves and tied neither to the other. How much of the start this queue explains stays open, since one execution of a_wsgdma was as short as the change. The forecast also left out the tenth load, `wsg4`, which came at 67.1 and cost 1.2 us of waiting: a wait for w_sg was one of its signs of being wrong.

**Behind `hv0.0`, -0.5.** It was -3.7, in parts of -6.5, +2.3, +0.7 and -0.4. The first has two causes: the collision at 86.77, which b_gm prices at 2.4 us in the profile and 3.1 by the runs, and TensorE's work that had moved ahead: 2.7 us less busy in that stretch (0.4 of it fillers), where the forecast let the moves cancel "within a microsecond". The collision at 97.42 is gone as well, and no run prices it; nor is it shown how the three add up. In the second stretch the new order waits for mask rows (TensorE's waits, 104 to 155 us):

```profile
PE PSC L781 <- DMA QA<-Dt: 1.8, 1, 1.8
PE PSC L781 <- DMA QB<-Dt: 0.6, 1, 0.6
```

Without the copies on VectorE it is up to 3.3 us longer still, as a_actevac shows, a fall of the clock included; the forecast gave them no price there.

**The rivals.** Collisions didn't turn up among the gating products (four on VectorE in that stretch, 0.71 us in the mean), but among the `vhat`: 2.1 us, all but 0.55 of it hidden behind `wsg4`. The clock did fall, to 0.64 from 17.8 to 22.0, a condition under which the forecast called itself wrong; it cost 1.25 us up to `hv0.0`, not 16. The range's lower end held the no-idle bound and one collision, but not the work moved ahead of `hv0.0` and nothing at all for the freed queue.
